# Attention on one core: from batch 1's third tile on, TensorE's queue keeps the written order

## The chip, the cores and the metric

The program runs on one core of a Trainium2 chip. The metric is the device time of one execution in microseconds (us). The kernel before took 511.47 us, the median of three runs (511.29 to 512.98).

## What is computed

Three layers follow each other, in 32-bit floating point, for two batches of 768 tokens.

- Attention, 8 heads of 64. Each query sees two sets of keys in one softmax: the keys less than 16 positions away, and 24 summaries, one for each block of 32 tokens. A summary's key is the block's elementwise maximum, its value the block's mean, and log(32) is added to its score.
- A gated feed-forward layer. Each token is mixed with the one before it, `xk = mu_k * x + (1 - mu_k) * x_prev` and likewise `xr`. The output is `sigmoid(xr @ w_r) * (relu(xk @ w_k)**2 @ w_v)`, with 512 to 1024 to 512 channels.
- A mixer. `relu(x.T @ w_tok1) @ w_tok2` over the tokens is added to x, and then `relu(u @ w_ch1) @ w_ch2` over the channels is added to u.

The weights arrive as 64-bit numbers. The kernel rounds them, and splits each operand of the large products into a high and a low part, so that each product is three matmuls: high by high, high by low, low by high.

## The kernel before

**Engines.** PE (TensorE) does all products and transposes. DVE (VectorE), ACT (ScalarE) and POOL (GpSimd) share the rest, and SP issues the DMAs. A tile is 128 queries of one batch; there are 6 for each batch. The profile names a product by the PSUM tile that it writes.

**One attention tile.** `s_stage` (L298) writes scores into `sp` (L309): 32 small matmuls, for 4 pairs of heads, 2 halves of the queries and 2 heads (e = 0, 1) of a pair, on 64 x 64 quarters of the array. The two heads of a pair lie in different rows of the array. DVE adds the mask and takes the row extreme (L327), ACT takes the exponential and its sum (L329). In batch 1, `n_stage` (L335) divides: DVE inverts the sum (L337, L338) and POOL scales P by it (L340), four operations for a head. `t_stage` (L343) transposes P on PE into `pt` (L346), 4 for each e, and copies it to `PT`. `v_stage` (L354) multiplies by the values into `pv` (L366), 32 small matmuls for both e, and ACT copies the result into `xT` (L374). In batch 0 the two e are separate units, P isn't divided; the values' result is, with a broadcast matmul `rb` (L382), and filler products `spin` (L556) run among the first units.

**The products beside it.** `main` (L523) is a generator with the feed-forward layer's first part. It goes through six chunks of 256 tokens. A chunk has four steps g. A step writes `ko` (L539: 8 groups of three matmuls of 256 columns), `k2_tile` (L485) squares and splits it (ACT rl L489, DVE L490, ACT kh L491, POOL kl L492), and `values` (L510) adds it into `acc`: 4 groups of three matmuls of 512 columns, written one step later, behind the next step's ko. Both use `mm3` (L472). In this text ko2.1 is the ko of chunk 2, step 1. A chunk can start when its two attention tiles are done: `make` (L500) then calls `mixed` (L459), with POOL tmp (L466), DVE xk (L467), ACT xh and DVE xl. `Weights.step` (L138) rounds one block of weights on ACT, DVE and POOL.

**How the two are woven.** `attention` (L390) is a generator too. Each of its yields hands over a cost; the loop at L609 turns it into credit, times 1.2 for the first 25 yields and 1.8 (`RATIO2`) after that, and takes groups of products from `main` until the credit is used up. A ko group costs 0.33 and an acc group 0.65. Batch 0 has 12 steps of one unit, batch 1 has 6 steps of one tile. In batch 1, step t writes the scores of tile t, then the division, transposes and values of tile t - 1 (`slots`, L404), and yields 1.9, 0.43, 0.43 and 1.4 between. The last transposes and values of batch 0 are written behind the first scores of batch 1.

**What sets the order.** The written order isn't the order on the engine. A planner simulates the program and fills each engine's queue: of what is ready by its simulation, it takes what has the highest priority. Priority is the written place; `ahead(n)` moves a function's instructions n places forward (transposes and values 400, `HT` and `HV`). On the chip each queue then runs in the planner's order. `behind` (L173) ties an instruction behind another in that order, without a wait. `in_line` (L168) uses it to chain the matmuls of one tile's scores, and of one tile's values, in batch 1, so that the two e alternate; other instructions can still come between. `mark` holds the last score matmul of each stage, and DMAs of inputs and weights are tied behind it (`after`, L179). Scores have two banks of PSUM (`s`), transposes two (`pt`), values one (`pv`), ko one and acc two.

Of the kernel before, what the change touches and what calls it, by code (L numbers as in the profile page):

```python
# [23 lines left out]
LAGS = 1, 2  # L24
LATE = (0,)
HOLD = 6.0
PEB, PTB, VB = 16, 3, 5
MW = 256
RATIO, NR, RATIO2 = 1.2, 25, 1.8
# [25 lines left out]
def fused_kernel(ctx, tc, q, k, v, vt, mu, w_k, w_v, w_r, w_t1, w_t2, w_c1, w_c2, out):  # L55
    nc = tc.nc
    B, NT = q.shape[:2]
# [10 lines left out]
    NC = NB + NK  # L68
# [13 lines left out]
    ident = const.tile([128, 128], F32, name="ident")  # L82
# [80 lines left out]
            return True  # L163

    mark = []
    line = []

    def in_line(inst):  # L168

        behind(inst, line[-1:])  # L170
        line.append(inst)

    def behind(inst, marks):  # L173

        for m in marks:
            tc.add_manual_dep(inst.ins, m.ins.name,
                              mybir.DependencyInfo(mybir.DependencyClass.NoSync, mybir.DependencyReason.DATA), reason="queue order")
# [32 lines left out]
    state = {}  # L210
# [22 lines left out]
    @ahead(HK)  # L233
    def kw_sums(b, t):
        st = state[b]
        for o in (0, WC - NB):
            nc.gpsimd.tensor_scalar(st["kw"][t][:, :, o:o + NB], st["ks"], 1.0, 1.0, ALU.mult, ALU.mult)
# [37 lines left out]
    def vw_sums(b, t):  # L275
        ahead(HV if b or t == 0 else 0)(copy_sums)(b, t)
# [20 lines left out]
    @ahead(HS)  # L297
    def s_stage(b, t, es):  # L298
        st = state[b]
        mask = masks[1 if t == 0 else 2 if t == NT - 1 else 0]  # L300
        kw, qT = st["kw"][t], st["qT"][t]
        sps = [bank("s", 2, [128, NP, NC], "sp") for _ in es]
        line.clear()
        for p in range(NP):
            for half in range(2):
                c0 = half * (WC - NC)
                for sp, e in zip(sps[::-1], es[::-1]):
                    r = slice(64 * e, 64 * e + 64)
                    m = nc.tensor.matmul(sp[64 * half:64 * half + 64, p], qT[r, p, 64 * half:64 * half + 64],  # L309
                                         kw[r, p, c0:c0 + NC], start=True, stop=True)  # L310
                    if len(es) > 1:
                        in_line(m)
        if PINL:
            mark.append(m)
        zs = []
        for sp, e in zip(sps, es):
            mn = at.tile([128, NP], F32, tag="mn", bufs=4, name="mn")
            if b not in LATE:
                den = at.tile([128, NP], F32, tag="den", bufs=4, name="den")
            else:  # L320
                if e == 0:
                    st["den"][t] = at.tile([128, 2, NP], F32, tag="dens", bufs=3, name="dens")
                den = st["den"][t][:, e]
            P = []
            for p in range(NP):
                pe = at.tile([128, NC], F32, tag="pe", bufs=PEB, name="pe")
                nc.vector.tensor_tensor_reduce(out=pe, in0=sp[:, p], in1=mask, op0=ALU.add, op1=ALU.min,  # L327
                                               scale=-1.0 / math.sqrt(D), scalar=3.0e38, accum_out=mn[:, p:p + 1])
                nc.scalar.activation(pe, pe, AF.Exp, bias=mn[:, p:p + 1], scale=-1.0, accum_out=den[:, p:p + 1])  # L329
                P.append(pe)  # L330
            zs.append({"u": (b, t, e), "P": P, "den": den})
        return zs
# [9 lines left out]
    @ahead(HT)  # L342
    def t_stage(z):  # L343
        pt = bank("pt", 2, [128, NP, 128], "pt")
        for p in range(NP):
            nc.tensor.transpose(pt[:NC, p], z["P"][p], ident)  # L346
        z["PT"] = at.tile([NC, NP, 128], F32, tag="PT", bufs=PTB, name="PT")
        if z["u"][::2] in PT_ACT:
            nc.scalar.copy(z["PT"], pt[:NC])
        else:  # L350
            nc.vector.tensor_copy(z["PT"], pt[:NC])

    @ahead(HV)
    def v_stage(zs):  # L354
        b, t, _ = zs[0]["u"]
        st = state[b]
        if t not in st["pv"]:
            st["pv"][t] = bank("pv", 1, [128, NP, 128], "pv")
        pv = st["pv"][t]
        line.clear()  # L360
        for p in range(NP):
            for half in range(2):
                for z in zs[::-1]:
                    e = z["u"][2]
                    h = 2 * p + e
                    m = nc.tensor.matmul(pv[64 * e:64 * e + 64, p, 64 * half:64 * half + 64],  # L366
                                         st["vw"][t][half][0][:, h * D:(h + 1) * D],
                                         z["PT"][:, p, 64 * half:64 * half + 64], start=True, stop=True)
                    if len(zs) > 1:
                        in_line(m)  # L370
        if zs[-1]["u"][2] == 1:
            c0 = b * XB + 1 + 128 * t
            if b not in LATE:
                nc.scalar.copy(xT[:, :, c0:c0 + 128], pv)  # L374
            else:
                den = st["den"].pop(t)
                nc.vector.tensor_scalar(den, den, 1e-9, None, ALU.add)
                nc.vector.reciprocal(den, den)
                rb = bank("pt", 2, [128, NP, 128], "rb")
                for p in range(NP):  # L380
                    for e in range(2):
                        nc.tensor.matmul(rb[64 * e:64 * e + 64, p], den[:, e, p:p + 1].to_broadcast([128, D]), ident,  # L382
                                         start=True, stop=True)
                x = xT[:, :, c0:c0 + 128]
                nc.scalar.copy(x, pv)
                nc.vector.tensor_tensor(x, x, rb, ALU.mult)

    done_tiles = [0]

    def attention():  # L390
        slots = {}
        n0 = 2 * NT
        steps = [(0, t, (e,)) for t in range(NT) for e in range(2)] + [(b, t, (0, 1)) for b in range(1, B) for t in range(NT)]
        for i in range(len(steps) + 1):
            if i < len(steps):
                b, t, es = steps[i]
                if b and t == 0:
                    yield from prep(b)
                zs = s_stage(b, t, es)
                if len(es) == 1:  # L400
                    for what, z, lag in zip((t_stage, v_stage), (zs[0], zs), LAGS):
                        slots.setdefault(min(i + lag, n0), []).append(((i + lag, lag), what, z))
                else:
                    slots[i + 1] = [((i, 1), n_stage, z) for z in zs] + [((i, 2), t_stage, z) for z in zs] + [((i, 3), v_stage, zs)]  # L404
                if i < SPIN_UNITS:
                    spin(SPIN)
                yield 0.95 * len(es)
                if es[-1] == 1 and t + 1 < NT:
                    kw_sums(b, t + 1)
                if t == 0 and es[-1] == 1 - b * (len(es) == 1):  # L410
                    if b == 0:
                        v_gather(b)
                    vw_sums(b, 0)
            for _, what, z in sorted(slots.get(i, ()), key=lambda s: s[0]):
                what(z)
                if what is t_stage:
                    yield 0.43
                elif what is v_stage:
                    yield 0.7 * len(z)
                    done_tiles[0] += len(z) / 2  # L420
            if i < len(steps):
                if 0 in es:
                    if t + 1 < NT and t + 1 not in state[b]["vw"]:
                        vw_load(b, t + 1)
                    if b and t + 2 < NT:
                        q_load(b, t + 2)
                if 1 in es and t + 1 < NT:
                    vw_sums(b, t + 1)
                if b + 1 < B:
                    for e in es:  # L430
                        prep_next(b + 1, 2 * t + e)

    def prep_next(b, j):

# [13 lines left out]
    def prep(b):  # L448

        for t in range(NT):  # L450
            k_max(b, t)
            yield HOLD / (NT + 2)
        for j in range(2):
            vt_sum(b, j)
            yield HOLD / (NT + 2)
        kw_sums(b, 0)
        v_gather(b)
# [14 lines left out]
    def mm3(o, pairs, first=True, last=True, cost=0.65):  # L472
        n = len(pairs)
        i = 0
        for (ah, al), (bh, bl) in pairs:
            for l, r in ((ah, bh), (ah, bl), (al, bh)):
                nc.tensor.matmul(o, l, r, start=(first and i == 0), stop=(last and i == 3 * n - 1))  # L477
                i += 1
            yield cost

# [98 lines left out]
    for kind in range(3):  # L579
        mc = const.tile([128, NC], F32, name=f"mask{kind}")  # L580
        mm = work.tile([128, 2, 128], F32, tag="t32", bufs=2, name="mm")
        for half in range(2):
            m = mm[:, half, :NC]
# [282 lines left out]
```

## Time and profile before

| | us |
|---|---|
| median of three runs | 511.47 |
| profiled execution, its own time | 511.19 |
| its span, first to last instruction | 509.40 |
| PE busy | 492.6 (97%) |
| DVE busy | 249.1 (49%) |
| ACT busy | 206.4 (41%) |
| POOL busy | 186.4 (37%) |

Attention fills the span up to some 178 us, woven with products from 51 us on. From there to about 255 us come the rest of the feed-forward layer and its gate (`ro`), and after that the mixer, which is PE alone for the most part. Matmuls are pipelined: the profile gives each a start and a modelled end, so the times of neighbours overlap, and the distance from one start to the next tells what a matmul costs.

### The profile page before, as it was taken

How to read it: one execution, taken by the hardware profiler on the slowest of the kernel's cores; microseconds unless marked ns; L12 is line 12 of the kernel's file. 1: busy time of each engine (PE TensorE's matmuls, PEld its weight loads, DVE VectorE, ACT ScalarE, POOL GpSimd, SP SyncE). 2: the span in 40 equal slices, each digit the busy share in tenths (PEclk: the TensorE clock that was granted, in tenths of full speed). 3: DMA queues.
4: the chain of work that ended last, by engine and by line, in shares of the span. 5: the costliest groups of instructions: out<-in, count | busy, mean ns of one | idle time of the engine just before them, and what ended most of it. 6: DMA issues, size and time to landing. Idle time of an engine off the chain costs nothing.

```text
span 509.4 us, 7950 instructions
## 1 busy us (share of the span) xinstructions
PE 492.6 (97%) x3064; PEld 399.6 (78%) x3064; DVE 249.1 (49%) x544; ACT 206.4 (41%) x477; POOL 186.4 (37%) x250
## 2 busy tenths in 40 slices
PE   7999897999999999999999999999999999999995
PEld 3578775788888888887888888888888888888884
DVE  3789999740515174798676576343141211311112
ACT  1689655962534444556455435343110201001000
POOL 5335567971534465697734333332100000000000
PEclk9999999999999999999999999999999999999999
DMA  8999942031000660001525650000020000200002
GB/s 254 307 295 338 333 128 71 9 100 40 21 0 14 237 248 0 1 0 42 164 85 209 235 176 1 0 1 1 0 84 0 1 0 1 82 1 0 0 1 82
DMA packets 24197, 45.40 MB, mean 89 GB/s; under 512 B 2112, under 2 KB 11328, under 8 KB 24160
## 3 DMA queue, kind: packets, MB, share of 16 engines
q1 hardware_dynamic: 24160, 44.90, 28.1%
q8 instruction: 24, 0.39, 0.3%
q14 instruction: 13, 0.11, 0.1%
HBM read 41.16 MB, written 3.15 MB: 87 GB/s over the span
## 4 chain that ended last, share of the span: by engine, by line
PE 79%; DVE 9%; POOL 4%; issue 3%; ACT 2%; DMA 2%; SPq 1%; DVEq 0%; POOLq 0%; ACTq 0%
PE o L791 19%; PE go L477 19%; PE ko L477 10%; PE acc L477 10%; PE ro L477 5%; PE ho L477 3%; PE h L477 3%; PE sp L309 3%; PE pv L366 2%; DVE xk L467 2%; PE pt L346 2%; DMA xT<-in_vt_dram 1%; PE spin L556 1%; DVE wf L152 1%; PE utr L745 1%
## 5 line engine op out<-in xcount | busy, mean ns | idle before, releaser
L477 PE MATMUL go<-u,w 128*128 128x512 f32 x432 | 106.7, 393 | 0.0
L161 POOL TENSOR_TENSOR w<-wf,w 128x512 fp32r<-128x512 f32 x50 | 68.7, 1379 | 85.5 <-ACT w L160 78.8
L477 PEld LDWEIGHTS go<-u,w 128*128 128x128 f32 x432 | 80.7, 188 | 17.5
L791 PE MATMUL o<-w,gh 128*128 128x512 f32 x288 | 89.0, 395 | 0.0
L706 DVE SCALAR_TENSOR_TENSOR gl<-go,gh 128x512 fp32r<-128x512 f32 x36 | 24.9, 691 | 121.1 <-ACT gh L705 120.9
L477 PE MATMUL ko<-xh,w 128*128 128x256 f32 x384 | 77.0, 289 | 0.7 <-ACT w L160 0.6
L705 ACT ACTIVATE gh<-go 128x512 fp32r<-128x512 f32 x36 | 21.5, 597 | 128.8 <-PE go L477 128.7
L477 PEld LDWEIGHTS ko<-xh,w 128*128 128x128 f32 x384 | 61.4, 188 | 4.5 <-issue 1.3
L791 PEld LDWEIGHTS o<-w,gh 128*128 128x128 f32 x288 | 54.0, 188 | 12.1
L477 PE MATMUL acc<-w,kh 128*128 128x512 f32 x192 | 60.7, 398 | 1.9 <-ACT kh L491 1.9
L477 PE MATMUL ko<-xl,w 128*128 128x256 f32 x192 | 54.6, 284 | 1.0 <-DVE xl L469 1.0
L791 PE MATMUL o<-w,gl 128*128 128x512 f32 x144 | 55.4, 394 | 0.0
L160 ACT CAST w<-wf 128x512 fp32r<-128x512 f32 x50 | 30.9, 619 | 47.3 <-DVE wf L158 47.1
L492 POOL TENSOR_TENSOR kl<-rl,kh 128x512 fp32r<-128x512 f32 x24 | 34.5, 1437 | 34.6 <-ACT kh L491 31.2
L466 POOL TENSOR_SCALAR tmp<-xT,oms 128x256 f32<-128x256 f32 x52 | 38.1, 742 | 23.1 <-DVE xk L467 15.0
L158 DVE SCALAR_TENSOR_TENSOR wf<-wst,wf 128x512 int32<-128x512 int32 x50 | 41.4, 834 | 8.4 <-ACT wst L148 6.9
L329 ACT ACTIVATE pe<-pe,mn 128x120 f32<-128x120 f32 x96 | 36.6, 383 | 18.5 <-DVE mn L327 18.2
L477 PEld LDWEIGHTS acc<-w,kh 128*128 128x128 f32 x192 | 34.6, 188 | 9.1 <-ACT kh L491 2.4
L490 DVE TENSOR_TENSOR rl<-rl 128x512 f32<-128x512 f32 x24 | 18.9, 785 | 46.7 <-ACT rl L489 46.3
L467 DVE SCALAR_TENSOR_TENSOR xk<-xT,mus,tmp 128x256 f32<-128x256 f32 x52 | 39.2, 784 | 4.2 <-POOL tmp L466 3.8
L477 PE MATMUL acc<-w,kl 128*128 128x512 f32 x96 | 37.1, 397 | 1.1 <-POOL kl L492 1.1
L477 PEld LDWEIGHTS ko<-xl,w 128*128 128x128 f32 x192 | 36.2, 189 | 2.1 <-DVE xl L469 1.3
(85 smaller groups left out, 695.2 us busy)
## 6 DMA issues: line engine op xcount, KB each, us to landing
wst<-in_moe_w_ch_dram SPq DMA_DIRECT2D x24, 512.0 KB, 4.6
wst<-in_moe_w_k_dram SPq DMA_DIRECT2D x8, 512.0 KB, 7.6
wst<-in_moe_w_v_dram SPq DMA_DIRECT2D x8, 512.0 KB, 10.3
kw<-in_k_dram SPq DMA_DIRECT2D x12, 320.0 KB, 8.8
wst<-in_moe_w_tok_dram SPq DMA_DIRECT2D x6, 512.0 KB, 4.5
out_dram<-o SPq DMA_DIRECT2D x12, 256.0 KB, 2.0
ybuf<-in_v_dram SPq DMA_DIRECT2D x12, 192.0 KB, 9.8
vw<-in_v_dram SPq DMA_DIRECT2D x12, 192.0 KB, 2.6
```

Source lines behind the costliest of these rows:

```text
L158: nc.vector.scalar_tensor_tensor(wi, top, 3, wi, ALU.logical_shift_left, ALU.bitwise_or)
L160: self.rounded.append(nc.scalar.copy(hi, wf))
L161: nc.gpsimd.tensor_tensor(lo, wf, hi.bitcast(F32), ALU.subtract)
L329: nc.scalar.activation(pe, pe, AF.Exp, bias=mn[:, p:p + 1], scale=-1.0, accum_out=den[:, p:p + 1])
L466: nc.gpsimd.tensor_scalar(tmp, xT[:, d, x0 - 1:x0 - 1 + MW], om[:, d:d + 1], 1.0, ALU.mult, ALU.mult)
L467: nc.vector.scalar_tensor_tensor(xk[:, d], xT[:, d, x0:x0 + MW], mu[:, d:d + 1], tmp, ALU.mult, ALU.add)
L477: nc.tensor.matmul(o, l, r, start=(first and i == 0), stop=(last and i == 3 * n - 1))
L490: nc.vector.tensor_tensor(rl, rl, rl, ALU.mult)
L492: nc.gpsimd.tensor_tensor(lo, rl, hi.bitcast(F32), ALU.subtract)
L705: nc.scalar.activation(hi, o, AF.Relu)
L706: nc.vector.scalar_tensor_tensor(lo, o, 0.0, hi.bitcast(F32), ALU.max, ALU.subtract)
L791: nc.tensor.matmul(acc[t], l, r, start=(f == 0 and i == 0), stop=(f == nf - 1 and i == 2))
```

## The change

Batch 0 and batch 1 get a loop each. Batch 0 keeps its order, and its last transposes and values are now written before the preparation of batch 1. In batch 1, tile t's step writes: the values of tile t - 1; the scores of tile t, with the loads for later tiles; a yield of `G1` = 3.0; the division and the transposes of tile t; a yield of `G2` = 1.5. `in_line` has a new meaning: while `pinned` is set, it ties an instruction behind the one written just before it on its engine. It is now called for scores, transposes, values and the products of `mm3`, and `pinned` is set from t = 2 (`PIN_T`) to the end of the loop, so the first pinned instructions are the values of tile 1. The chain within tiles 0 and 1 is gone.

```diff
@@ -24,6 +24,8 @@
 LAGS = 1, 2
 LATE = (0,)
 HOLD = 6.0
+PIN_T = 2
+G1, G2 = 3.0, 1.5
 PEB, PTB, VB = 16, 3, 5
 MW = 256
 RATIO, NR, RATIO2 = 1.2, 25, 1.8
@@ -163,12 +165,12 @@
             return True
 
     mark = []
-    line = []
+    pinned = [False]
 
     def in_line(inst):
 
-        behind(inst, line[-1:])
-        line.append(inst)
+        if pinned[0]:
+            tc.keep_in_program_order(inst)
 
     def behind(inst, marks):
 
@@ -300,7 +302,6 @@
         mask = masks[1 if t == 0 else 2 if t == NT - 1 else 0]
         kw, qT = st["kw"][t], st["qT"][t]
         sps = [bank("s", 2, [128, NP, NC], "sp") for _ in es]
-        line.clear()
         for p in range(NP):
             for half in range(2):
                 c0 = half * (WC - NC)
@@ -308,8 +309,7 @@
                     r = slice(64 * e, 64 * e + 64)
                     m = nc.tensor.matmul(sp[64 * half:64 * half + 64, p], qT[r, p, 64 * half:64 * half + 64],
                                          kw[r, p, c0:c0 + NC], start=True, stop=True)
-                    if len(es) > 1:
-                        in_line(m)
+                    in_line(m)
         if PINL:
             mark.append(m)
         zs = []
@@ -343,7 +343,7 @@
     def t_stage(z):
         pt = bank("pt", 2, [128, NP, 128], "pt")
         for p in range(NP):
-            nc.tensor.transpose(pt[:NC, p], z["P"][p], ident)
+            in_line(nc.tensor.transpose(pt[:NC, p], z["P"][p], ident))
         z["PT"] = at.tile([NC, NP, 128], F32, tag="PT", bufs=PTB, name="PT")
         if z["u"][::2] in PT_ACT:
             nc.scalar.copy(z["PT"], pt[:NC])
@@ -357,7 +357,6 @@
         if t not in st["pv"]:
             st["pv"][t] = bank("pv", 1, [128, NP, 128], "pv")
         pv = st["pv"][t]
-        line.clear()
         for p in range(NP):
             for half in range(2):
                 for z in zs[::-1]:
@@ -366,8 +365,7 @@
                     m = nc.tensor.matmul(pv[64 * e:64 * e + 64, p, 64 * half:64 * half + 64],
                                          st["vw"][t][half][0][:, h * D:(h + 1) * D],
                                          z["PT"][:, p, 64 * half:64 * half + 64], start=True, stop=True)
-                    if len(zs) > 1:
-                        in_line(m)
+                    in_line(m)
         if zs[-1]["u"][2] == 1:
             c0 = b * XB + 1 + 128 * t
             if b not in LATE:
@@ -390,45 +388,59 @@
     def attention():
         slots = {}
         n0 = 2 * NT
-        steps = [(0, t, (e,)) for t in range(NT) for e in range(2)] + [(b, t, (0, 1)) for b in range(1, B) for t in range(NT)]
-        for i in range(len(steps) + 1):
-            if i < len(steps):
-                b, t, es = steps[i]
-                if b and t == 0:
-                    yield from prep(b)
-                zs = s_stage(b, t, es)
-                if len(es) == 1:
-                    for what, z, lag in zip((t_stage, v_stage), (zs[0], zs), LAGS):
-                        slots.setdefault(min(i + lag, n0), []).append(((i + lag, lag), what, z))
-                else:
-                    slots[i + 1] = [((i, 1), n_stage, z) for z in zs] + [((i, 2), t_stage, z) for z in zs] + [((i, 3), v_stage, zs)]
+        for i in range(n0 + LAGS[-1]):
+            if i < n0:
+                t, e = divmod(i, 2)
+                (z,) = s_stage(0, t, (e,))
+                for what, arg, lag in zip((t_stage, v_stage), (z, [z]), LAGS):
+                    slots.setdefault(i + lag, []).append((lag, what, arg))
                 if i < SPIN_UNITS:
                     spin(SPIN)
-                yield 0.95 * len(es)
-                if es[-1] == 1 and t + 1 < NT:
-                    kw_sums(b, t + 1)
-                if t == 0 and es[-1] == 1 - b * (len(es) == 1):
-                    if b == 0:
-                        v_gather(b)
-                    vw_sums(b, 0)
+                yield 0.95
+                if e and t + 1 < NT:
+                    kw_sums(0, t + 1)
+                if i == 1:
+                    v_gather(0)
+                    vw_sums(0, 0)
             for _, what, z in sorted(slots.get(i, ()), key=lambda s: s[0]):
                 what(z)
                 if what is t_stage:
                     yield 0.43
-                elif what is v_stage:
-                    yield 0.7 * len(z)
-                    done_tiles[0] += len(z) / 2
-            if i < len(steps):
-                if 0 in es:
-                    if t + 1 < NT and t + 1 not in state[b]["vw"]:
+                else:
+                    yield 0.7
+                    done_tiles[0] += 0.5
+            if i < n0:
+                if e == 0 and t + 1 < NT and t + 1 not in state[0]["vw"]:
+                    vw_load(0, t + 1)
+                if e and t + 1 < NT:
+                    vw_sums(0, t + 1)
+                prep_next(1, i)
+        for b in range(1, B):
+            yield from prep(b)
+            zs = []
+            for t in range(NT + 1):
+                pinned[0] = t >= PIN_T
+                if t:
+                    v_stage(zs)
+                    done_tiles[0] += 1
+                if t < NT:
+                    zs = s_stage(b, t, (0, 1))
+                    if t + 1 < NT:
+                        kw_sums(b, t + 1)
                         vw_load(b, t + 1)
-                    if b and t + 2 < NT:
+                    if t == 0:
+                        vw_sums(b, 0)
+                    if t + 2 < NT:
                         q_load(b, t + 2)
-                if 1 in es and t + 1 < NT:
-                    vw_sums(b, t + 1)
-                if b + 1 < B:
-                    for e in es:
-                        prep_next(b + 1, 2 * t + e)
+                    yield G1
+                    for z in zs:
+                        n_stage(z)
+                    for z in zs:
+                        t_stage(z)
+                    if t + 1 < NT:
+                        vw_sums(b, t + 1)
+                    yield G2
+            pinned[0] = False
 
     def prep_next(b, j):
 
@@ -474,7 +486,7 @@
         i = 0
         for (ah, al), (bh, bl) in pairs:
             for l, r in ((ah, bh), (ah, bl), (al, bh)):
-                nc.tensor.matmul(o, l, r, start=(first and i == 0), stop=(last and i == 3 * n - 1))
+                in_line(nc.tensor.matmul(o, l, r, start=(first and i == 0), stop=(last and i == 3 * n - 1)))
                 i += 1
             yield cost
```

## Rows read from the trace of the kernel before

**Rows 1.** The windows view, six stretches; columns as its first line names them.

```profile
core 0: us, PE busy (x) PEld busy (x) DVE busy (x) ACT busy (x) POOL busy (x), PEclk, DMA share, GB/s
...
78.00:96.00 18.00, 14.70 (x126) 10.55 (x125) 16.14 (x64) 13.13 (x45) 15.38 (x22) 1.00 0.20 56
96.00:178.00 82.00, 82.00 (x729) 70.00 (x730) 29.06 (x98) 40.31 (x113) 40.15 (x63) 1.00 0.20 64
178.00:255.00 77.00, 75.88 (x429) 65.86 (x428) 56.26 (x71) 41.26 (x67) 53.96 (x47) 1.00 0.23 76
```

**Rows 2.** The waits view of PE, 60 to 96 us: total, times, longest.

```profile
PE acc L477 <- ACT kh L491: 1.9, 2, 1.0
...
PE ko L477 <- ACT w L160: 0.6, 1, 0.6
```

**Rows 3.** The timeline of PE, batch 1's scores: start, us, line, out<-in, count.

```profile
90.57 0.42 PE L309 MATMUL sp<-kw,qT 64*64 64x120 f32 x2
...
103.07 0.43 PE L309 MATMUL sp<-kw,qT 64*64 64x120 f32 x6
...
129.30 0.40 PE L477 MATMUL acc<-w,kl 128*128 128x512 f32 x1
129.63 0.63 PE L309 MATMUL sp<-kw,qT 64*64 64x120 f32 x14
130.19 0.39 PE L477 MATMUL ko<-xh,w 128*128 128x256 f32 x1
130.42 0.27 PE L477 MATMUL ko<-xl,w 128*128 128x256 f32 x1
...
162.97 0.40 PE L477 MATMUL acc<-w,kl 128*128 128x512 f32 x1
163.29 0.43 PE L309 MATMUL sp<-kw,qT 64*64 64x120 f32 x6
163.65 0.39 PE L477 MATMUL ko<-xh,w 128*128 128x256 f32 x1
163.88 0.28 PE L477 MATMUL ko<-xl,w 128*128 128x256 f32 x1
```

**Rows 4.** The timeline of PE, the values of batch 1's third tile.

```profile
114.99 0.39 PE L477 MATMUL ko<-xh,w 128*128 128x256 f32 x1
115.31 0.33 PE L366 MATMUL pv<-PT,vw 120*64 120x64 f32 x2
...
116.14 0.50 PE L477 MATMUL ko<-xh,w 128*128 128x256 f32 x2
```

**Rows 5.** The timeline of PE, scores of one head and of both.

```profile
45.51 1.04 PE L309 MATMUL sp<-kw,xT 64*64 64x120 f32 x16
...
71.97 1.03 PE L309 MATMUL sp<-kw,qT 64*64 64x120 f32 x26
```

**Rows 6.** The chain that ended last (start, us, what): values, products.

```profile
27.13 1.07 PE pv L366 x16
...
176.09 1.08 PE pv L366 x32
...
180.21 2.78 PE acc L477 x12
183.00 2.85 PE ko L477 x24
```

**Rows 7.** The timeline of POOL behind the last scores of batch 1.

```profile
166.32 3.38 POOL L340 TENSOR_SCALAR pe<-pe,den 128x120 f32<-128x120 f32 x8 [2.30 <-DVE den L338]
```

**Rows 8.** The groups view, 95 to 178 us: busy us, mean ns, idle.

```profile
L492 POOL TENSOR_TENSOR kl<-rl,kh 128x512 fp32r<-128x512 f32 x12 | 16.5, 1376 | 27.0 <-ACT kh L491 27.0
...
L466 POOL TENSOR_SCALAR tmp<-xT,oms 128x256 f32<-128x256 f32 x14 | 8.3, 604 | 6.6 <-ACT xT L374 4.7 <-DVE xk L467 1.9
...
L489 ACT ACTIVATE rl<-ko 128x512 f32<-128x512 f32 x11 | 6.6, 597 | 17.1 <-PE ko L477 17.1
```

**Rows 9.** The page's DMA issues: count, KB each, us to landing.

```profile
vw<-in_v_dram SPq DMA_DIRECT2D x12, 192.0 KB, 2.6
```

## The prediction

> **What bounds the kernel now.** I read the windows view first. In the 82 us from 96 to 178, PE is busy for all 82.00, at a granted clock of 1.00 (its 2.4 GHz level), while DVE, ACT and POOL are busy 29 to 40 us each. From 78 to 96 PE has 14.70 of 18.00, so 3.3 us are idle, and there DVE (16.14) and POOL (15.38) are the full engines [rows 1]. The waits view says the same: before 96 PE waits for products' inputs (1.9 us for ACT's kh, 0.6 us for a rounded weight) [rows 2]; for 96 to 178 it lists no wait of PE at all. Batch 1's third to sixth tiles lie almost wholly in that dense stretch. So the change cannot win by removing waits there: there are none. What is left is how PE's busy time is spent. A busy PE is not a PE at its peak, so I went to the timeline and read start to start. There the scores of those four tiles come as 14 pieces instead of 4, the first at 90.57, the last at 163.29 [rows 3].
>
> **Gain 1: pieces of scores.** From the start of the last acc product before a piece to the start of the second ko product behind it: 130.42 - 129.30 = 1.12 us with 14 score products between, 163.88 - 162.97 = 0.91 us with 6 [rows 3]. Without a piece the same two starts lie 0.35 apart: one acc (2.79 us for 12, 0.232) and one ko (2.85 for 24, 0.119) [rows 6]. So a piece of 14 costs 0.77 and one of 6 costs 0.56: 0.026 for each score product and 0.40 for coming and going. Pinned, a tile's 32 scores are one piece: 0.40 + 32 x 0.026 = 1.24. Ten pieces go, 10 x 0.40 = **4.0 us**. Some of the ten touch transposes or values, where one of the two changes is paid anyway; at 0.30 each for those the bound is 3.0, and 4.4 above.
>
> By the Trainium skill ("TensorE: Matmul & The Clock Gate", Part 1, engine queue depths) TensorE can pull weight loads ahead of running matmuls, out of a partial reorder window. If that hid the change from full-array products to the scores' 64 x 64 tiles, a piece would cost nothing to enter and leave; the trace disagrees, with 0.40 us a piece [rows 3]. By that rule gains 1 to 3 would be nil; it is a rival below.
>
> **Gain 2: values of the third tile.** They were cut into 28, 2 and 2 with a ko product between. From 114.99 to 116.14, 1.15 us hold 2 ko (0.24) and 4 values (1.08 us for 32, so 0.14) [rows 4, 6]: **0.8 us** lost, and pinned that goes (0.6 to 0.8).
>
> **Gain 3: values and scores adjoin.** In the written order a tile's values are followed at once by the next tile's scores, so one return to the products falls away, at half of 0.40, for four tiles: at most 0.8. The change from values to scores is itself unseen in my rows, so 0 is the other end. I take **0.4**. By the Trainium skill ("TensorEngine Tiling (Array Packing)", Key Properties) a change of tiling mode drains the engine, and values (120 rows) and scores (64 rows) are two modes; by it this gain is 0 and the sum 0.4 less.
>
> Transposes stay eight a tile; some now stand singly between ko products. I count 0 for gathering them, 0.40 a tile at most if each such tile saved a piece's fixed cost.
>
> **Price 1: tiles 0 and 1 lose their chain.** Before, the chain kept the two heads alternating. One head alone takes as long for half the work: 16 scores 1.04 us against 1.03 for 26 [rows 5], 16 values 1.07 against 1.08 for 32 [rows 6]. Unpaired, a tile's scores cost about 0.8 more (two tiles), the values 1.1 (tile 0 only; tile 1's values are already pinned). Ends 0 and 2.7. Both heads mostly become ready together, and the planner then takes them as written, so I take **0.8**.
>
> **Price 2: work that ran early.** PE took tile 2's scores from 90.57 and had finished tile 3's by 103.5 [rows 3], while products lagged. Pinned, they stand behind the first half of chunk 2's first values product (acc2.0). If products cannot take their place, PE loses two tiles' scores (2.5), a tile's values (1.3) and four transposes (0.4): 4.2. If they can, 0. After 96 PE never waits [rows 1], so products are to be had; before 96 lies one tile's scores, 1.24. The aux engines are relieved of two tiles at the same time. I take **1.2**.
>
> **Price 3: pinned transposes wait.** The chain from a tile's last score to its last scaled P: scores end at 163.65 [rows 3], POOL scales from 166.32 to 169.70 [rows 7], 6.05 us. The cover is the products that G1 pays for, 3.0 x 1.8 = 5.4 units, as whole groups of three (0.33 a ko group, 0.65 an acc group; 0.356 and 0.697 us by [rows 6]). Following both generators by hand gives after the scores of tile 2: 2 acc, 8 ko, 3 acc = 6.3 us; tile 3: 3 ko, 4 acc, 6 ko = 6.0; tile 4: 1 acc, 8 ko, 3 acc = 5.6; tile 5: 1 ko, 4 acc, 7 ko = 5.6. The first head's transposes come first and need only half of POOL's scaling. So bare, the waits are 0, 0.1, 0.4 and 0.4. But a k2 chain can lie in front: POOL's kl 1.38 us, ACT's rl 0.60, and mixing's tmp 0.60 [rows 8]. Queued behind a waiting transpose is everything on PE, products included; and behind those the k2 chains. Low end 0 (the first head's transposes fill), high end kl + tmp on each of four tiles, 1.38 + 0.60 - 0.25 of slack = 1.7, so 6.9. I take **1.2**. From transposes to values G2 pays 2.7 units, about 2.9 us, against a PT copy, an ACT pass of the size of rl's 0.60 [rows 8]: free; without that cover 0.6 a head.
>
> **Edits at nothing.** vw_load and q_load now stand before the transposes; their DMAs on SP's queue still follow the tile's scores, and the values come a whole tile (about 12 us) later, against 2.6 us to landing [rows 9]; uncovered, 2.6 a tile. vw_sums' DMAs stay behind the transposes, a tile ahead of use. kw_sums on POOL are long done. Batch 0's last transposes and values now precede the preparation of batch 1 instead of following batch 1's first scores: the same instructions; by the idle of that stretch, at most 3.3 either way [rows 1], and I take 0. The yields pay 4.5 units a tile for 4.16, so 3.9 units more products are written before the end of attention and fewer behind it: moved, not added. The DMAs of the next stage's weights stand behind the last scores, 163.65 before; my sum puts those within 2 us of it. From 178 on PE has 75.88 of 77.00 [rows 1]: little to win, the same work.
>
> **Sum.** Gains 4.0 + 0.8 + 0.4 = 5.2; prices 0.8 + 1.2 + 1.2 = 3.2; net 2.0 us. The profiled execution took 511.19 (span 509.40 and 1.79 around it), so 509.2; the median of the runs shown, 511.47, lies 0.28 above it, and on the median I forecast **509.5**.
>
> **Rivals.**
> *More: the early idle goes too.* With tiles 2 and 3 off DVE, ACT and POOL, weights and k2 chains finish sooner and 3.3 us of idle [rows 1] fall with price 2: 5.2 + 3.3 - 0.8 - 1.2 = 6.5 off, 505.0. For it: DVE and POOL are full there. Against: tiles 0 and 1, batch 0's end and the weights still crowd there, and the deferred work only starts at 90.57 [rows 3].
> *Same: prices eat the gain.* At 2.0 for each of prices 1 and 2 and 1.2 for price 3, 511.5. For it: each has an upper end that high.
> *Slower: the pinned PE waits at its transposes.* Place: the first transposes of tiles 2 to 5. Price: 1.7 a tile, 6.9, with the other two prices 2.0: 511.5 - 5.2 + 8.9 = 515.2. It decides once the four waits together pass 3.2, 0.8 a tile. For it: POOL's chain is 6.05 against a cover of 5.6 to 6.3, with no slack. Against: 29 to 40 us of work in 82 leave the three engines half empty [rows 1].
> *Slower: no filler.* Price 2 at 4.2 and price 1 at 2.7 with 1.2: 2.9 over, 514.4.
> *The pin does not save anything.* If a piece were free (the rule on weight loads above), only prices stand: 511.5 + 3.2 = 514.7. The rows speak against it.
>
> **How the numbers follow.** What a measurement here can tell from no change is about 0.3%, 1.5 us: faster means under 509.9, slower over 513.0. Forecast 0.43 (its own range 507.5 to 511.0; 0.34 of it faster, 0.09 same); more 0.16, faster; same 0.18; waits at transposes 0.13, no filler 0.07, free pieces 0.03, all slower. Faster 0.50, same 0.27, slower 0.23. The range 505.3 to 514.5 leaves out about half of the gain rival and of the slower ones.
>
> **What would show it.** In the profile after: batch 1's last four tiles have one piece of scores each, right behind the values, and values uncut (gains 1 to 3; if pieces remain, the pin does less than said). PE's waits list transposes behind POOL's pe: under 2 us in total fits price 3, over 3 us is the slower rival. Idle of PE between 78 and 96 over 4.5 us shows price 2, under 1 us the first rival. Groups of 16 scores in tiles 0 and 1 show price 1. If the last values of batch 1 end before about 175 with PE still dense, the gain is where I put it; if they do and the end does not move, it was given back after 178, which I have not foreseen.

## The result: slower, 519.2 us

The changed kernel took 519.21 us, the median of four runs (517.65 to 519.63), against 511.47: a ratio of 1.0141, 95% interval 1.0124 to 1.0158. The forecast was 509.5 and its range ended at 514.5, so sign and range were both wrong.

The profiled execution of the changed kernel took 519.63 (span 517.80), that of before 511.19 (509.40). I cut both spans at four events on PE that mean the same in each kernel: ko0.0 begins; ko1.0 begins; batch 1's attention and acc3.2 have both ended; the last `ho` (the mixer's second product; `h` is its first) has ended. Stretch lengths in us, for kernels of the experiments too:

| kernel | A: to ko0.0 | B: to ko1.0 | C: to end of attention and acc3.2 | D: to end of ho | E: rest | span |
|---|---|---|---|---|---|---|
| before | 51.3 | 44.7 | 86.8 | 119.5 | 207.1 | 509.4 |
| after | 53.1 | 46.7 | 87.4 | 123.6 | 207.0 | 517.8 |
| e6, units as before | 50.7 | 47.2 | 88.9 | 119.7 | 207.1 | 513.6 |
| e9, both yields | 51.5 | 46.7 | 89.4 | 119.5 | 207.0 | 514.1 |
| e4, lag and pin | 52.5 | 43.2 | 86.1 | 119.4 | 207.1 | 508.3 |
| e12, lag, pin, adjoining | 51.1 | 43.3 | 85.0 | 119.4 | 207.1 | 505.8 |

Of the 8.4 us, 4.1 lie in D, where nothing was edited. C should have become 4.0 shorter (gains 5.2, price 3 1.2) and became 0.6 longer. B is 2.0 longer, which is what prices 1 and 2 came to together. A is 1.8 longer in this execution only: its instructions are the same, and the kernels e6 and e3, which share them, have 50.7 and 51.1. In it TensorE's granted clock was 0.72 from 16 to 22 us, against 1.00 before (rows in the last section).

The windows view, first of before in the stretches C and D (D in two parts, at the first `h`), then of after in B (from 79 us) to D. The columns are those of [rows 1].

```profile
96.00:182.80 86.80, 86.80 (x758) 74.31 (x759) 31.60 (x102) 43.17 (x118) 40.51 (x64) 1.00 0.24 78
182.80:255.50 72.70, 71.58 (x401) 61.81 (x400) 54.21 (x68) 38.89 (x64) 53.60 (x47) 1.00 0.19 61
255.50:302.30 46.80, 46.80 (x212) 38.28 (x212) 30.56 (x52) 22.72 (x39) 17.29 (x14) 1.00 0.51 178
```

```profile
79.00:99.80 20.80, 16.84 (x134) 13.55 (x134) 12.79 (x53) 13.86 (x47) 18.26 (x26) 0.92 0.18 50
99.80:187.20 87.40, 83.45 (x753) 73.05 (x753) 29.23 (x109) 41.30 (x112) 37.67 (x57) 1.00 0.19 57
187.20:262.00 74.80, 71.72 (x401) 61.50 (x400) 52.92 (x68) 39.25 (x64) 52.82 (x49) 1.00 0.28 92
262.00:311.00 49.00, 47.53 (x214) 38.57 (x214) 36.65 (x57) 24.62 (x43) 20.38 (x16) 1.00 0.45 157
```

In C, PE was busy for all 86.80 us before, and now for 83.45 of 87.40: 3.35 us less, and 3.95 us of idle that were not there. In D the work is the same (118.4 and 119.3) and the idle went from 1.12 to 4.55.

The waits view of PE after, whole run (total, times, longest), says for what:

```profile
PE pt L346 <- POOL pe L340: 3.8, 6, 1.5
PE ko L489 <- POOL w L163: 2.9, 3, 1.7
PE ro L489 <- ACT xh L480: 2.7, 2, 1.8
...
PE ho L489 <- DVE gl L718: 1.5, 1, 1.5
```

The timeline of PE after shows values and scores of tiles 1 and 2, the transposes of tile 4, and the three waits of D:

```profile
132.37 1.15 PE L365 MATMUL pv<-PT,vw 120*64 120x64 f32 x32
133.45 1.05 PE L310 MATMUL sp<-kw,qT 64*64 64x120 f32 x32
134.43 0.73 PE L489 MATMUL acc<-w,kh 128*128 128x512 f32 x2
...
166.25 1.09 PE L346 MATMUL pt<-ident,pe 128*120 128x128 f32 x5
168.84 0.32 PE L346 MATMUL pt<-ident,pe 128*120 128x128 f32 x1 [1.50 <-POOL pe L340]
169.34 0.32 PE L346 MATMUL pt<-ident,pe 128*120 128x128 f32 x1 [0.18 <-POOL pe L340]
169.84 0.33 PE L346 MATMUL pt<-ident,pe 128*120 128x128 f32 x1 [0.18 <-POOL pe L340]
169.93 0.71 PE L489 MATMUL acc<-w,kh 128*128 128x512 f32 x2
...
222.99 1.19 PE L489 MATMUL ro<-w,xh 128*128 128x512 f32 x4 [1.78 <-ACT xh L480]
...
261.25 0.73 PE L489 MATMUL ro<-w,xh 128*128 128x512 f32 x2 [0.96 <-ACT xh L480]
...
282.61 0.50 PE L489 MATMUL ho<-gl,w 128*128 128x512 f32 x1 [1.47 <-DVE gl L718]
```

The 14 pieces of [rows 3] have become four, each 32 scores in 0.98 us right behind 32 values in 1.08: the edit does what it says. But tile 4's eight transposes take 3.68 us from the first to the product behind them (169.93 - 166.25), as the last three come one by one as POOL scales their P. The timelines of DVE and of POOL after show why so late:

```profile
160.85 1.09 DVE L479 SCALAR_TENSOR_TENSOR xk<-xT,mus,tmp 128x256 f32<-128x256 f32 x2 [3.00 <-POOL tmp L478]
161.86 0.27 DVE L327 CUSTOM_DVE_ANT_0 pe<-sp,mask 128x120 f32<-128x120 f32 x1
```

```profile
164.05 1.11 POOL L478 TENSOR_SCALAR tmp<-xT,oms 128x256 f32<-128x256 f32 x2 [1.30 <-DVE xk L479]
165.13 4.66 POOL L340 TENSOR_SCALAR pe<-pe,den 128x120 f32<-128x120 f32 x8
```

Scores ended at 160.5, P was whole at 169.8: 9.3 us, where I had 6.05. Of the 3.2 us more, 1.9 lie ahead of the scaling, which starts 4.6 us behind the scores' end against 2.7 in [rows 7]. Chunk 4's mixing is in the way mostly on DVE: its `xk` runs first, so that the row extremes start 1.35 us behind the scores. On POOL its `tmp` ends at 165.13, and the first `den` is ready at 164.94, so that `tmp` by itself held the scaling for 0.2 us. The other 1.3 us are the eight scalings, 4.66 us here against 3.38 in [rows 7]; why they are slower, no run shows. Start to start the four tiles' transposes take 2.42, 1.35, 3.68 and 1.67 us, 9.12 in all; eight that wait for nothing take 0.80 (tile 3 in the kernel e3 below, 152.79 to 153.59). So by this count the waits cost 9.12 - 4 x 0.80 = 5.9 us, a little more than gains 1 to 3 were to bring. The waits view counts only the idle in them, 3.8.

### The profile page after: what moved, and what is told of

It is laid out like the page before. It is cut to its first block, busy times and chain, and to the rows that moved or that the text cites. A ratio compares the mean times of both kernels' runs of the same rounds, so it can differ in the third digit from the quotient of the medians.

```text
span 517.8 us, 7944 instructions
## 1 busy us (share of the span) xinstructions
PE 492.2 (95%) x3064; PEld 400.9 (77%) x3064; DVE 246.6 (48%) x544; ACT 206.6 (40%) x477; POOL 185.9 (36%) x250
## 4 chain that ended last, share of the span: by engine, by line
PE 54%; DVE 5%; issue 2%; ACT 2%; POOL 2%; DMA 0%; DVEq 0%; POOLq 0%; ACTq 0%
PE o L803 19%; PE go L489 19%; PE ho L489 3%; PE h L489 3%; PE ro L489 3%; PE acc L489 3%; PE ko L489 2%; DVE xk L479 2%; PE utr L757 1%; ACT xh L480 1%; DVE wf L160 1%; POOL kl L504 1%; DVE xl L481 1%; POOL tmp L478 1%; DVE wf L154 1%
## 5 line engine op out<-in xcount | busy, mean ns | idle before, releaser
L163 POOL TENSOR_TENSOR w<-wf,w 128x512 fp32r<-128x512 f32 x50 | 67.2, 1346 | 83.4 <-ACT w L162 76.6
L489 PE MATMUL acc<-w,kh 128*128 128x512 f32 x192 | 59.2, 398 | 0.0
L504 POOL TENSOR_TENSOR kl<-rl,kh 128x512 fp32r<-128x512 f32 x24 | 31.9, 1328 | 44.0 <-ACT kh L503 32.5
L478 POOL TENSOR_SCALAR tmp<-xT,oms 128x256 f32<-128x256 f32 x52 | 40.9, 795 | 14.4 <-DVE xk L479 11.5
L479 DVE SCALAR_TENSOR_TENSOR xk<-xT,mus,tmp 128x256 f32<-128x256 f32 x52 | 36.9, 736 | 12.6 <-POOL tmp L478 12.6
```

The source lines that it names most:

```text
L163: nc.gpsimd.tensor_tensor(lo, wf, hi.bitcast(F32), ALU.subtract)
L478: nc.gpsimd.tensor_scalar(tmp, xT[:, d, x0 - 1:x0 - 1 + MW], om[:, d:d + 1], 1.0, ALU.mult, ALU.mult)
L479: nc.vector.scalar_tensor_tensor(xk[:, d], xT[:, d, x0:x0 + MW], mu[:, d:d + 1], tmp, ALU.mult, ALU.add)
L489: in_line(nc.tensor.matmul(o, l, r, start=(first and i == 0), stop=(last and i == 3 * n - 1)))
L504: nc.gpsimd.tensor_tensor(lo, rl, hi.bitcast(F32), ALU.subtract)
```

## Experiments

Theories at the start: the pinned transposes wait; the products written early are missing later ("late"); against them the lost chain, the moved end of batch 0, and the pin as such. Every time is a median on a chip where before took 511.5 to 511.7; brackets are 95% intervals of the ratio to before.

**The order without its pin, and the pin from tile 4 on.**

```diff
-PIN_T = 2
+PIN_T = 99
```

That is e1; e5 has 4 in place of 99.

> The changed kernel with the pin never set (PIN_T = 99): the new written order is left to the planner. Three theories of the 7.7 us. Waits (the pinned PE waits at its transposes, 5.6 us in the profile after): the transposes move freely again, about 513, with scores in pieces again. Filler (tiles 2 and 3 can no longer run early, so PE idles before 100 us): they can again, about 512. Order (the rewritten loop itself costs, whatever the pin does): stays at 517 or more.

> The changed kernel with PIN_T = 4: pinned from the values of tile 3 on, tiles 2 and 3 free. Waits: the waits at the transposes of tiles 4 and 5 stay (3.6 us of the 5.6), about 517. Filler: tiles 2 and 3 run early again and the idle before 100 us falls, about 514. Order: 519.

Measured: e1 516.39 [1.0066, 1.0148], e5 518.56 [1.0096, 1.0189]. The rewritten order costs 4.9 us with no pin at all; the pin adds 2.8. So the loss is mostly in what the order says, not in that it is kept. The order includes the two yields: e1 hands over 4.5 units a tile as well, and its PE waits 1.5 us for gl in D.

**The chain put back** in all tiles of batch 1 (the new order, no pin, `in_line` called as before the change).

```diff
+    line = []
...
-        if pinned[0]:
-            tc.keep_in_program_order(inst)
+        behind(inst, line[-1:])
+        line.append(inst)
```

> The changed kernel's written order without the pin (as in the run at PIN_T = 99, 516.4), with the old chain back in batch 1's scores and values. What is left of the loss without the pin, some 4.9 us, has three candidates. Chain (heads left unpaired): back to about 513. Batch 0's end (now written ahead of batch 1's preparation) or late (waits of PE behind the last attention tile, for xh and gl): stays at 516.

Measured: 523.45 [1.0194, 1.0266], 7 us over e1. Its tiles 2 and 3 have scores in 5 and 6 pieces, and tile 2's values come in 12. So putting the chain back doesn't mend the new order. Since it covers all six tiles here, and without the pin, the run doesn't price the lost pairing of tiles 0 and 1 by itself.

**Batch 0's end where it was**, behind batch 1's first scores.

```diff
-        for i in range(n0 + LAGS[-1]):
+        for i in range(n0):
...
+                    if t == 0:
+                        for i in range(n0, n0 + LAGS[-1]):
+                            for _, what, z in sorted(slots.get(i, ()), key=lambda s: s[0]):
+                                what(z)
```

> The changed kernel with the last transposes and values of batch 0 written behind the first scores of batch 1 again, as before. Batch 0's end: the stretch up to 100 us is as before but for tile 2's scores, PE no longer waits near 77 us, and 2 to 3 us go: 516 to 517. Late, chain: 519. Since 3.3 more units are handed over, the late waits may move.

Measured: 519.82 [1.0107, 1.0183], no change. ko1.0 starts at 96.15, 3.7 us earlier, but with tile 0's values and tile 1's transposes still to do, and nothing of it is left at the end of C. This edit costs nothing, as I had it.

**Later transposes** (more products ahead of them).

```diff
-G1, G2 = 3.0, 1.5
+G1, G2 = 4.0, 0.5
```

> The changed kernel with G1 = 4.0 and G2 = 0.5: the same units for a tile, but 1.8 units (1.9 us) more products between a tile's scores and its transposes. Waits: the 5.6 us at the transposes mostly go, about 514, and PE's waits list under 1 us for transposes behind POOL. Filler: 519, since tiles 2 and 3 still stand behind acc2.0. Order: 519.

Measured: 515.25 [1.0051, 1.0097], 4.0 us under after. In the timeline of PE of e3, the transposes of tiles 2 to 4 and what follows:

```profile
140.22 1.24 PE L346 MATMUL pt<-ident,pe 128*120 128x128 f32 x8
141.22 0.36 PE L489 MATMUL ko<-xh,w 128*128 128x256 f32 x1
...
152.79 1.04 PE L346 MATMUL pt<-ident,pe 128*120 128x128 f32 x8
153.59 0.71 PE L489 MATMUL acc<-w,kh 128*128 128x512 f32 x2
...
165.00 1.35 PE L346 MATMUL pt<-ident,pe 128*120 128x128 f32 x8
166.11 0.36 PE L489 MATMUL ko<-xh,w 128*128 128x256 f32 x1
```

They are whole groups of eight, 1.00, 0.80 and 1.11 us start to start, with no wait in brackets. Tile 4's scores end at 156.72 here, so the cover was 8.3 us, where the changed kernel had 5.7. The waits were worth about 4 us of the total.

**The units of before**: 4.16 a tile instead of 4.5.

```diff
-G1, G2 = 3.0, 1.5
+G1, G2 = 3.0, 1.16
```

> The changed kernel with G2 = 1.16 for 1.5, so that a tile hands over 4.16 units as before and 3.7 units of products stay behind the attention. Late: the waits of PE after the last values of batch 1 (2.7 us for xh, 1.5 for gl) go, 515 to 516. Batch 0's end, chain: no change, 519. Transposes still wait.

Measured: 515.36 [1.0043, 1.0097], 3.9 us under after. Stretch D, by the windows view of e6:

```profile
186.80:259.60 72.80, 71.79 (x401) 61.82 (x400) 54.69 (x71) 39.56 (x65) 54.55 (x47) 1.00 0.22 73
259.60:306.50 46.90, 46.90 (x213) 38.28 (x213) 30.65 (x52) 22.77 (x39) 17.52 (x14) 1.00 0.50 178
```

119.7 us with 1.01 of idle, as before; the waits for xh and gl are gone, those at the transposes are not. Products that are written earlier are not just moved. By the waits view of PE from 186 to 310 us, e3 and e7, at 4.5 units a tile, wait for xh (2.5 and 2.7 us) and for gl (1.5) like the changed kernel, at 223, 261 and 283 us there; e6, e8 and e9, at 4.16, wait for neither. So the yields decide it. That the gate and the mixer need these products beside ACT's and DVE's work is my reading, and not shown step by step.

**Both, on two bases**: e8 is e7 with G1, G2 = 3.6, 0.56; e9 is the changed kernel with

```diff
-G1, G2 = 3.0, 1.5
+G1, G2 = 4.0, 0.16
```

> The changed kernel with batch 0's end as before and G1, G2 = 3.6, 0.56: transposes later by 1.08 units, 4.16 units a tile as before. If the waits at transposes, batch 0's end and the late waits are the loss, 509 to 511, near the old order with the pin alone (510.4). If the chain in tiles 0 and 1 or tiles 2 and 3 held back are a large part, 513 or more.

> The new order as it stands, but the two yields are 4.0 and 0.16 instead of 3.0 and 1.5: four units of products ahead of the transposes, and 4.16 units a tile as before the change. Theory: two prices made the change slower, the pinned transposes' waits (about 4 us, as the run with 4.0 and 0.5 gave back) and the products missing behind attention, which leave the gate and the mixer to wait (about 3.9 us, as the run with 3.0 and 1.16 gave back). They are separate, so both come back: 519.2 - 4.0 - 3.9 = 511.3 us, between 509.5 and 513. No wait of TensorE for x's gate behind attention, no transpose that waits over 1 us. Rival: both mends take back the same microseconds, or a pinned product waits for kl in the place of the transposes, as it did for 3.0 us with 3.6 and 0.56: 514.5 to 516.5, with acc3.0 or its neighbour waiting over 2.5 us for POOL's kl.

Measured: e8 516.26 [1.0049, 1.0102], e9 516.34 [1.0065, 1.0124]. The theory's 511.3 failed, and the rival's 514.5 to 516.5 held: the two mends do not add up. In e9 the waits behind attention are gone (D is 119.5) and PE waits elsewhere in C. The timelines of PE and of POOL of e9:

```profile
167.03 0.50 PE L489 MATMUL acc<-w,kl 128*128 128x512 f32 x1 [3.00 <-POOL kl L504]
```

```profile
161.12 4.64 POOL L340 TENSOR_SCALAR pe<-pe,den 128x120 f32<-128x120 f32 x8
165.72 1.26 POOL L504 TENSOR_TENSOR kl<-rl,kh 128x512 fp32r<-128x512 f32 x1
```

Now a pinned product stands at the head of PE's queue and waits 3.0 us for its `kl`, which POOL makes behind tile 4's scaling; from 165 to 175 us, at the end of that wait and behind it, the granted clock is below 1.00 (0.74 and 0.92 in two windows of 5 us). POOL serves both chains: in the changed kernel the scaled P is late, in e9 the kl. In e3 neither is late in C, so this is no rule of the order.

**The transposes alone not pinned.**

```diff
-            in_line(nc.tensor.transpose(pt[:NC, p], z["P"][p], ident))
+            tp = nc.tensor.transpose(pt[:NC, p], z["P"][p], ident)
+            if not pinned[0]:
+                in_line(tp)
```

> The new order with its yields of 3.0 and 1.5, and the four tiles' transposes alone not pinned: values, scores and products keep the written order. Theory (transposes at the head of a queue that must keep its order are what waits): the 5.6 us of their waits go, less one or two microseconds for products that are cut by them, so 515 to 517 us, and no wait of a transpose over 0.5 us; the waits behind attention stay, since the units are unchanged. Rival (PE would have waited for the scaled scores in any order, since the values of the tile are due): values wait instead, time within 1 us of 519.2.

Measured: 519.32 [1.0119, 1.0171]: no gain. The rival's time is right and its reason is not: the transposes still wait, in the waits view of e11 for 96 to 190 us:

```profile
PE pt L346 <- POOL pe L340: 3.6, 5, 1.5
```

Left free, they stand in the same places as before, tile 4's three late ones too; only tile 3's are cut by two ko products. So price 3 is due to where the transposes are written, and not to their own pin.

**The pin with the old lag.** e4 is the kernel before, with its loop, its chain in tiles 0 and 1, and its lag (tile t's division, transposes and values written behind tile t + 1's scores); only the pin is added, to scores, transposes, values and products. e10 sets it one tile earlier (t >= 1).

```diff
     def in_line(inst):
-        behind(inst, line[-1:])
-        line.append(inst)
+        if pinned[0]:
+            tc.keep_in_program_order(inst)
+        else:
+            behind(inst, line[-1:])
+            line.append(inst)
...
+                pinned[0] = b > 0 and t >= 2
...
+            pin(nc.tensor.transpose(pt[:NC, p], z["P"][p], ident))
```

> The kernel before, its loop and its lag of one tile kept, with the pin alone added from batch 1's third step on (scores, transposes, values and products). Transposes stand a whole tile behind their scores here. Waits: no waits are left and the gain of whole pieces stays, 507 to 511. Filler: tiles 2 and 3 still can't run early, so 513 to 516. Order: the old loop with whole pieces, under 509.

> The loop of before, with its lag of one tile between scores and transposes, pinned from batch 1's second tile on (the run that gave 510.35 us was pinned from its third). Theory: the pin is worth what it saves in pieces: S1.1 in one piece instead of two or three saves about 0.8 us, and nothing waits since the transposes lie a tile behind, so 509.5 to 510.5 us. Rival: the pin so early holds TensorE in the stretch 60 to 96 us, where products are not yet ready to fill it, and the time goes to 512 to 518, as pinning the new order from its fourth tile on moved that one by under 1 us.

Measured: e4 510.35 [0.9918, 0.9979]; e10 511.14 [0.9971, 1.0028]. In e4 the scores of tiles 2 to 5 are four pieces, and for 96 to 182 us the waits view of its PE has only

```profile
PE pv L375 <- ACT PT L358: 1.2, 3, 0.5
PE ko L488 <- ACT rl L500: 0.3, 1, 0.3
```

So the pin is worth something where a tile of other work lies between scores and transposes. A pin one tile earlier is no better.

**Lag and adjoining.** In e12 the yield of 1.4 behind a pinned tile's values moves ahead of them, so that they adjoin the scores of the tile after next.

```diff
+                late = what is v_stage and pinned[0]
+                if late:
+                    yield 1.4
                 what(z)
...
-                    yield 0.7 * len(z)
+                    if not late:
+                        yield 0.7 * len(z)
```

> The loop of before with its lag of a tile, pinned from batch 1's third tile on (the run that gave 510.35 us), and the yield of 1.4 that stood behind a tile's values moved ahead of them: the values of tile t-1 adjoin the scores of tile t+1, and scores, transposes and values keep a tile's distance from each other's operands. It joins the new order's one cheap point (adjoining, no product between) with the lag of before. Theory: three visits of TensorE to the small tiles fewer at 0.40 us are 1.2 us, nothing waits at the transposes, since scaled scores still have a tile to be ready: 508.5 to 510 us. Rival: the values come 1.4 units later (about 4 us), so the buffers of a tile's values and the writing of the attended x come later and stand in POOL's and the DMA queues' way, and the gain is given back behind attention: 510.5 to 513 us, with a wait of a product for xl or kl over 1.5 us that the earlier run had not.

Measured: **507.67 us** (507.17 to 508.46) [0.9901, 0.9933], faster than both kernels. The windows view of C in e4 and then in e12, and the timeline of e12's PE for the values of tile 3 and the scores of tile 5:

```profile
95.80:181.80 86.00, 84.82 (x792) 74.60 (x793) 30.43 (x112) 44.14 (x119) 40.79 (x68) 1.00 0.25 85
94.40:179.40 85.00, 84.22 (x793) 75.03 (x794) 29.89 (x110) 43.43 (x118) 42.63 (x67) 1.00 0.24 76
```

```profile
156.42 1.15 PE L375 MATMUL pv<-PT,vw 120*64 120x64 f32 x32
157.50 1.05 PE L318 MATMUL sp<-kw,qT 64*64 64x120 f32 x32
```

By these rows C is 1.0 us shorter than in e4: PE's busy time fell by 0.60 and its idle by 0.40. PE leaves the products for the small tiles and comes back three times less. The expected 0.40 a visit would be 1.2 of busy time; 0.60 is 0.2 a visit, the "half of 0.40" of gain 3. (The medians lie 2.7 apart, the two spans 2.5. Of these 1.4 are in A, where the granted clock from 16 to 22 us was 0.72 in e4 and 1.00 in e12, and so not of this edit.) The eight scalings of tile 4 take 4.55 us here as well, and nothing waits for them.

## Why the prediction was wrong

*What bounds the kernel.* Right: PE's busy time in C, with no waits to win. What follows from "no waits" I did not draw: a stretch that is 100% busy shows that the old order hides every chain, not that another order would.

*Gains 1, 2 and 3*: right in kind. Four pieces, uncut values, adjoining; PE's work in C fell by 3.35 us beside 5.2 forecast, a sum that also holds what moved across C's ends, so that the sizes of gains 1 and 2 are not measured apart. For gain 3, e12 shows 0.2 a visit in PE's busy time, the upper end of what I had, and its low end of 0 is refuted. The Trainium skill's rule that weight loads are pulled ahead of running matmuls ("TensorE: Matmul & The Clock Gate", Part 1) would have made those visits free if it covered a change of shape; e12 disagrees with its 0.60 us for three, as [rows 3] did.

*Prices 1 and 2*: their sum of 2.0 is what B lost (1.98), but the reasons are borne out in part at most. The sign of price 1 is there for tile 1, whose scores come as 16 at 81.62 us and 16 at 85.39; tile 0's are 30 and 2, paired. What that cost, no run tells: the chain put back made the whole worse (e2). With tiles 2 and 3 held back as in price 2, e4's B is 1.5 us shorter than before, about what the 32 scores take that it leaves to C (1.24), and its C is shorter too. Idle from 79 to 99.8 is 3.96 us, under the 4.5 that was to show price 2. What B lost is open: from 60 to 100 us PE waits mostly for rounded weights (2.9 us) and kl (1.6), its granted clock was 0.68 from 80 to 85 us, where before had 1.00 (up to 1.6 us, last section), and e7, whose B is 44.1, gains nothing in the end.

*Price 3* failed: 5.9 us where I took 1.2. It was the mechanism of the rival "the pinned PE waits at its transposes", whose condition (over 3.2 us) was met, and I gave it 0.13. Two terms were mis-sized. The chain is no constant 6.05: [rows 7] shows POOL's scaling with nothing of the next chunk's mixing ahead, and after the change it was 9.3 at tile 4. And the argument against, that POOL is half empty, is an average; the mixing, the kl and the scaling come in the same few microseconds. e3 gave 4.0 us of it back.

*Edits at nothing* failed at "moved, not added": the extra products, 3.7 units (0.34 x 6 x 1.8; the prediction has 3.9) and priced 0, cost 4.1 us in D. e6 took them out and D was back at 119.7. I had looked at D for idle to win (75.88 of 77.00) and not for what keeps it so dense: it is dense only as long as enough products are left for it. The last sentence of the prediction names this as what I had not foreseen. The rest of that paragraph holds (e7).

*Sum.* 509.5 + 4.7 (price 3) + 4.1 (yields) = 518.3 of 519.2. The two are the sizes in this kernel and no independent costs, since e9 gets 2.9 us of them back. The 509.5 has 2.0 for prices 1 and 2 in it, which B did lose, for reasons that stay open. Why PE waits for kl in e9 and not in e3, which differs from it by 0.34 units a tile, I did not settle.

*Rivals.* The slower one had the right place and, at 515.2, only half of the loss; no rival held the other half. "The pin does not save anything" is refuted by e4 and e12.

## What to carry to other kernels

An order that is kept needs lag: before pinning an in-order queue, measure for each consumer the longest time from its producer's start to its end over all tiles, not in one clean place, and write at least that much other work between; here 5.7 us were not enough, 8.3 us were just enough at the transposes (e3, which still lost 3.7 us in all), and a lag of a tile left no wait there (e4, where tile 2's scores end at 125.1 and its transposes begin at 140.6). Independent work that fills gaps was a stock here: spent earlier, it was missing later, in a stretch whose little idle was the sign that it covered something. Keep the lag and take the cheap part, adjoining visits to the small tiles.

## What the hardware showed that I had not expected

The granted clock falls to its lower level (1.2 GHz, 0.50 in the column) for some microseconds in places where PE had been idle in parts. The windows view of e1, with PE's busy time first and the granted clock after POOL's column:

```profile
75.00:80.00 5.00, 3.31 (x32) 2.55 (x31) 4.62 (x21) 3.25 (x12) 5.00 (x6) 1.00 0.00 0
80.00:85.00 5.00, 3.88 (x27) 2.46 (x27) 4.96 (x17) 4.67 (x15) 4.38 (x7) 1.00 0.33 77
85.00:90.00 5.00, 4.98 (x32) 4.38 (x31) 2.74 (x13) 4.18 (x19) 5.00 (x7) 0.55 0.35 123
90.00:95.00 5.00, 5.00 (x25) 3.28 (x23) 2.01 (x6) 1.21 (x2) 3.73 (x9) 0.50 0.00 0
95.00:100.00 5.00, 5.00 (x23) 3.94 (x24) 2.41 (x20) 3.42 (x17) 4.33 (x10) 0.59 0.00 0
```

PE was idle for 2.8 of the 10 us from 75 to 85, and then ran some 14 us at the lower level, 100% busy and at half speed, so that busy time alone shows nothing. That execution took 520.33 beside a median of 516.39. The same shows in the kernels compared above, before from 16 to 22 us first, then after:

```profile
16.00:22.00 6.00, 5.67 (x46) 3.24 (x46) 5.19 (x33) 5.02 (x25) 0.20 (x1) 1.00 1.08 311
```

```profile
16.00:22.00 6.00, 5.67 (x34) 3.05 (x36) 4.50 (x27) 4.52 (x23) 0.20 (x1) 0.72 1.07 315
...
80.00:85.00 5.00, 5.00 (x31) 4.30 (x31) 5.00 (x22) 5.00 (x20) 4.38 (x5) 0.68 0.17 41
```

As an estimate from these rows, 0.28 of 6 us and 0.32 of 5 us are up to 1.7 and 1.6 us of PE's time, most of A's 1.8 and of B's 2.0. Before had 1.00 in both places. So a part of the difference between the two profiled executions is the clock's. It is not the whole story of B: e12, the fastest, has 0.89 from 79 to 94.4 and a shorter B than before. Single executions show the size too: of before's in the experiments, those with a mean granted clock of 0.998 took 511.0 to 512.2 us and those with 0.992 took 513.2 to 513.5; the changed kernel's four had 0.987 to 0.993. Whether the new order's waits bring the clock down or chance does, no run separates.
